# Two heads per tile in an attention backward kernel: 16 KB rows, and gradients written over their inputs

## The chip, the cores and the metric

The kernel runs on one core of a Trainium2 chip. A core has a matrix engine (TensorE, "PE" in the profile; its weight loads stand apart as "PEld"), a vector engine (VectorE, "DVE"), a scalar engine (ScalarE, "ACT"), GpSimd ("POOL") and SyncE ("SP"). Each runs its own list of instructions in order and waits on semaphores. Transfers between HBM and the on-chip memory (128 partitions) are issued here from SP and POOL, and a few from ACT; 16 DMA engines carry them all. The metric is the device time of one execution in microseconds: before the change the median of three runs is 402.32 us (402.08 to 402.48).

## The reference

The program is the forward and backward pass of a decode step: one query token attends over a cache of 32 heads, 4096 keys and 128 features per head, in parallel with a dense layer with a Mish activation, and a gate mixes the two. All arrays are bf16. Cut to what matters:

```python
def _A_ref(x, k_cache, v_cache, wq, wo):      # attention of one token
    q = (x @ wq).reshape(B, Sq, H, Dh).transpose(0, 2, 1, 3)
    scores = einsum("bhqd,bhkd->bhqk", q, k_cache) * (Dh ** -0.5)
    p = softmax(scores, axis=-1)
    o = einsum("bhqk,bhkd->bhqd", p, v_cache)
    return o.transpose(0, 2, 1, 3).reshape(B, Sq, H * Dh) @ wo

def _B_ref(x, w1, b1, w2):                    # dense layer: mish(x w1 + b1) w2
    h = x @ w1 + b1
    return (h * tanh(softplus(h))) @ w2

g = sigmoid((x * gate_w).sum(-1, keepdims=True))
out = g * _A_ref(A_x, K, V, wq, wo) + (1 - g) * _B_ref(B_x, w1, b1, w2)
# outputs: out, and the gradients of A_x, K, V, wq, wo, w1, b1, w2, gate_w
```

K and V are 32 MB each (32 heads of 1 MB), and so are their gradients dK and dV. dK of a head is the outer product of the vector ds (one number per key) with the query; dV is the outer product of the probabilities p with the gradient of the head's output. The weights wq and wo (5.2 MB each), w1 and w2 (2.2 MB each) are read, and gradients of their sizes are written.

## The kernel before, in words

**Tiles.** One head is one tile: 128 partitions, each holding J = 32 consecutive keys of 128 features, an unbroken row of 8 KB in HBM (the views `Kv`, `Vv`, `dKv`, `dVv`, L65 to L68). The pool `kv_in` has four K and four V tiles, the pool `outs` five tiles for dK and dV.

**The loop** (L749) goes over the 32 heads. `period(h)` (L645) does one head, and computes the scores of head h + 1 at its end. K and V come with the keys on the partitions, so each is turned by TensorE: `transposes` (L575) turns four blocks of 128x128 (bf16 pairs moved as f32) into a PSUM tile `tr`, and ScalarE copies it to `tT` (L582); `products` (L585) multiplies the result with the query (scores, tile `sA`) or with the output gradient (dP, tile `sB`). Then the softmax: `reduce_max` (L664), a transposition to spread the maximum (L668), `negM` (L670), the exponentials `e` (L675), their sum (L678, L680), `rz`, its reciprocal (L682), and `p_bf` (L684). `o_part` (L660) gives the head's output; `part`, `dd` and `ds` (L691 to L702) give the gradient of the scores; L713 gives the gradient of the query.

**dK and dV** are made by VectorE in `outer` (L602), half a head per instruction, four instructions per head: `dv_half(h, ...)` in the head's own period, `dk_half(h - 1, ...)` in the first part of the next one. After the second half the tile is stored, from POOL's queue (`ring`, L115), and by SP for the last two heads. Four dV tiles go out by `spread` (L637), in pieces of unequal partition counts.

**The order of the loads** is SP's list. At the start: wq, wo, K and V of the first three heads, w1, two parts of w2. Then, at the head of each pass of the loop, `load_k(h + 3)` and `load_v(h + 3)` (L757, L758): such a load waits until the tile's last reader is done. wo of the next groups of four heads and wq of the next eight are loaded from the same list (L753, L756).

**Everything else** (preparing a group of four heads in `prep_steps`, closing it in `finish_steps`, the dense layer in `mlp_steps`) is cut into steps with a kind: "P" mostly TensorE, "D" VectorE, "T" small. `slot` (L254), called three times per head, takes the first steps of the list whose predecessors were done in an earlier slot, two of kind P and one or two of kind D. This order is fixed when the program is built. At the end, the gradient of wq is made in five pieces (`dwq_make`, L729), in tiles of `kv_in`; the gradient of w1 is stored when head 31 is loaded (L759).

Of the kernel before, what the change touches and what calls it, by code (L numbers as in the profile page):

```python
# [16 lines left out]
def kernel(  # L17
# [25 lines left out]
    P = 128  # L43
# [3 lines left out]
    J = Sk // P  # L47
# [10 lines left out]
    CH = [(0, 5), (5, 9), (9, FCN)]  # L58
# [6 lines left out]
    Kv = A_k_cache.rearrange("b h (p j) d -> (b h) p j d", p=P)  # L65
    Vv = A_v_cache.rearrange("b h (p j) d -> (b h) p j d", p=P)
    dKv = out_2.rearrange("b h (p j) d -> (b h) p j d", p=P)
    dVv = out_3.rearrange("b h (p j) d -> (b h) p j d", p=P)  # L68
# [16 lines left out]
    KB, VB = 4, 4  # L85
    const = ctx.enter_context(tc.tile_pool(name="const", bufs=1))
    kv_in = ctx.enter_context(tc.tile_pool(name="kv_in", bufs=KB))
    outs = ctx.enter_context(tc.tile_pool(name="outs", bufs=5))
# [26 lines left out]
    def ring(h):  # L115
        return nc.sync if h >= H - 2 else nc.gpsimd

    def load_k(h):
        if h < H:
            kts[h] = kv_in.tile([P, J, Dh], BF16, name="Kn", tag="Kn", bufs=KB)  # L120
            nc.sync.dma_start(kts[h][:], Kv[h])

    def load_v(h):
        if h < H:
            vts[h] = kv_in.tile([P, J, Dh], BF16, name="Vn", tag="Vn", bufs=VB)
            nc.sync.dma_start(vts[h][:], Vv[h])
# [13 lines left out]
    def load_w2(c):  # L140
        a, b = CH[c][0], min(CH[c][1], FM)
        w2cs[c] = mlp.tile([P, 5, D], BF16, name="w2c", tag="w2c", bufs=2)
        nc.sync.dma_start(w2cs[c][:, 0:b - a, :], w2_v[:, a:b, :])
# [4 lines left out]
    load_v(0)  # L148
    load_k(1)
    load_v(1)  # L150
    load_wo(1)
# [6 lines left out]
    load_k(2)  # L158
    load_v(2)
# [3 lines left out]
    load_w2(1)  # L163

# [74 lines left out]
    for i in range(3):  # L239
        t = const.tile([P, 2, G, 2, 2], BF16, name=f"qd2_{i}")  # L240
        nc.gpsimd.memset(t[:], 0.0)
        qds.append(t)
    junk = const.tile([P, WG * Dh], BF16, name="junk")
# [25 lines left out]
    def prep_steps(g, head):  # L269
# [15 lines left out]
        def qbc():  # L285
            wq = wqs[g // 2]
            q_ps = gr_ps.tile([P, GD], F32, name="q_ps", tag="gr")
            for rc in range(RC):
                nc.tensor.matmul(q_ps[:], lhsT=x_bf[:, rc:rc + 1].to_broadcast([P, P]),  # L289
                                 rhs=wq[:, rc, off:off + GD], start=(rc == 0), stop=(rc == RC - 1))  # L290
            gp["qd"] = wts.tile([P, 2, GD], BF16, name="qd", tag="qd")
            nc.scalar.copy(gp["qd"][:, 0, :], q_ps[:])

        def dbc():
            d_ps = gr_ps.tile([P, G, P], BF16, name="d_ps", tag="gr")
            bcast_rows(d_ps, gp["do4b"], G)
            nc.scalar.copy(gp["qd"][:, 1, :].rearrange("p (a i) -> p a i", i=G), d_ps[:].rearrange("p i a -> p a i"))

        def qdcol():
            c_ps = gp["qdc"] = gr_ps.tile([P, 2, G], F32, name="c_ps", tag="gr")  # L300
            for w in range(2):
                for hh in range(G):
                    nc.tensor.matmul(c_ps[:, w, hh:hh + 1], lhsT=gp["qd"][:, w, hh * Dh:(hh + 1) * Dh],
                                     rhs=ident_bf[:, 0:1], start=True, stop=True)
# [7 lines left out]
        def x2():  # L312
# [5 lines left out]
            nc.scalar.mul(t[0:hf, :, :, :, 0], x2[0:hf], scale)  # L318
            nc.scalar.mul(t[hf:P, :, :, :, 1], x2[hf:P], scale)
# [78 lines left out]
    def mlp_steps():  # L398
# [107 lines left out]
        def dh_cast():  # L506
            m["dh_bf"] = T("dh_bf", BF16)
            nc.vector.tensor_copy(m["dh_bf"][:], m["dh"][:])
            m["dh_bc"] = mlp.tile([P, F], BF16, name="dh_bc", tag="dh_bc")
# [36 lines left out]
        for c in range(NCH):  # L546
# [5 lines left out]
            add(f"dw2a_{c}", "D", dw2_part(c, a, a + 3), (f"badd{c}",) + tuple(f"dh_{fc}" for fc in range(a, b)), H0)  # L552
            add(f"dw2_{c}", "D", dw2_part(c, a + 3, b), (f"dw2a_{c}",), H0)
# [10 lines left out]
        add("dhc", "T", dh_cast, (f"dh_{FCN - 1}",), H0)  # L564
        add("dhb0", "P", dh_bc_part(0), ("dhc",), H0)
        add("dhb1", "P", dh_bc_part(1), ("dhc",), H0)
        for rc in range(RC):
            for k in range(2):
                add(f"dxm{rc}_{k}", "D", dx_part(rc, k), ("dhb0", "dhb1"), H0)
            add(f"dw1_{rc}", "D", dw1_part(rc), (f"dxm{rc}_1",), H0)  # L570

# [13 lines left out]
    def products(out, tb, c, vec):  # L585
        for t in range(4):
            k = c * 4 + t
            for par in range(2):
                nc.tensor.matmul(out[:, 2 * k:2 * k + W], lhsT=tb[:, t, par, :],  # L589
                                 rhs=vec[:, par, :].unsqueeze(1).to_broadcast([P, W // 2, 2]),  # L590
                                 start=(par == 0), stop=(par == 1))

    def k_chunk(h, c, ts):
        ts.append(transposes(kts[h], c))

    def s_chunk(h, c, ts):
        gp = gps[h // G]
        if c == 0:
            sts[h] = {"A": sa_ps.tile([P, 512], F32, name="sA", tag="sA")}
        products(sts[h]["A"][:, 0:J + W], ts[c], c, gp["x2"][:, 0, h % G])  # L600

    def outer(dst, col, row, half):  # L602
        n = J // 2
        a, b = half * n, (half + 1) * n
# [6 lines left out]
    def dk_half(h, half):  # L611
        if h < 0:
            return
        st = sts[h]
        if half == 0:
            st["dK"] = outs.tile([P, J, Dh], BF16, name="dK_sb", tag="dVK")
        outer(st["dK"], st["ds"], gps[h // G]["qd"][:, 0, (h % G) * Dh:(h % G + 1) * Dh], half)
        if h == H - 1:
            a, b = half * (J // 2), (half + 1) * (J // 2)
            ring(h).dma_start(dKv[h][:, a:b, :], st["dK"][:, a:b, :])  # L620
        elif half == 1:
            ring(h).dma_start(dKv[h], st["dK"][:])  # L622
        if half == 1:
            sts.pop(h)

    def dv_half(h, half):
        st = sts[h]
        if half == 0:
            st["dV"] = outs.tile([P, J, Dh], BF16, name="dV_sb", tag="dVK")
        outer(st["dV"], st["p"], gps[h // G]["qd"][:, 1, (h % G) * Dh:(h % G + 1) * Dh], half)  # L630
        if half == 1:
            if h % 7 == 5 and h < H - 3:
                spread(h // 7, dVv[h], st["dV"])
            else:
                ring(h).dma_start(dVv[h], st["dV"][:])  # L635

    def spread(i, dst, t):  # L637
        src = t[:].rearrange("p j d -> p (j d)")
        out = dst.rearrange("p j d -> p (j d)")
        if i % 3 == 0:  # L640
            nc.gpsimd.inc_swdge_sem([], [], mode="reset_dge_cursor")
        for a, b in (((120, 125), (0, 120), (125, 128)), ((0, 14), (14, 119), (119, 128)), ((0, 8), (8, 128)))[i % 3]:
            nc.gpsimd.dma_start(out[a:b, :], src[a:b, :], max_dma_last_dim=J * Dh)

    def period(h):  # L645
        gp = gps[h // G]
        st = sts[h]
        nxt = h + 1 < H
        A = st["A"]
        S, Z, O, MM = A[:, 0:J], A[:, 96:96 + J], A[:, 128:128 + W], A[:, 256:384]  # L650
        B = st["B"] = sb_ps.tile([P, 512], F32, name="sB", tag="sB")
        DP, DQ, PT = B[:, 0:J + W], B[:, 128:128 + W], B[:, 256:384]
        vec = gp["x2"][:, 1, h % G]
        tv, tk = [], []
        V = lambda c: tv.append(transposes(vts[h], c))
        dP = lambda c: products(DP, tv[c], c, vec)

        def o_part(a, b):
            for j in range(a, b):
                nc.tensor.matmul(O, lhsT=vts[h][:, j, :], rhs=st["e"][:, j:j + 1].to_broadcast([P, W]),  # L660
                                 start=(j == 0), stop=(j == J - 1))

        m32 = small.tile([P, 1], F32, name="m32", tag="m32")
        nc.vector.reduce_max(m32[:], S, axis=AX.X)  # L664
        V(0)
        dk_half(h - 1, 0)
# [3 lines left out]
        nc.vector.tensor_reduce(negM[:], MM, axis=AX.X, op=ALU.max, negate=True)  # L670
        dk_half(h - 1, 1)
        e = st["e"] = small.tile([P, J], BF16, name="e_bf", tag="e_bf")
        V(2)
        dP(0)
        nc.scalar.activation(e[:], S, ACT.Exp, bias=negM[:], scale=1.0)  # L675
        V(3)
        dP(1)
        nc.tensor.matmul(Z, lhsT=ones_bf[:], rhs=e[:], start=True, stop=True)  # L678
        zs = small.tile([P, 1], F32, name="zs", tag="zs")
        nc.vector.reduce_sum(zs[:], Z, axis=AX.X)  # L680
        rz = st["rz"] = small.tile([P, 1], F32, name="rz", tag="rz")
        nc.vector.reciprocal(rz[:], zs[:])  # L682
        p_bf = st["p"] = small.tile([P, J, 2], BF16, name="p_bf", tag="p_bf")
        nc.scalar.activation(p_bf[:], e[:].unsqueeze(2).to_broadcast([P, J, 2]), ACT.Copy, scale=rz[:])  # L684
        dP(2)
        o_part(0, J)
        dP(3)
        slot(h)
        part = small.tile([P, 1], F32, name="part", tag="part")
        pj = small.tile([P, J], F32, name="pj", tag="pj", bufs=1)  # L690
        nc.vector.scalar_tensor_tensor(pj[:], in0=DP[:, 0:J], scalar=1.0, in1=e[:], op0=ALU.mult, op1=ALU.mult,  # L691
                                       accum_out=part[:])
        dv_half(h, 0)
        nc.tensor.transpose(PT, part[:].to_broadcast([P, P]), ident_f[:])  # L694
        if nxt:
            k_chunk(h + 1, 0, tk)
            k_chunk(h + 1, 1, tk)
        dd = small.tile([P, 1], F32, name="dd", tag="dd")
        dj = small.tile([P, P], F32, name="dj", tag="dj", bufs=1)
        nc.vector.tensor_scalar(dj[:], PT, rz[:], None, ALU.mult, ALU.add, accum_out=dd[:])  # L700
        ds = st["ds"] = small.tile([P, J, 2], BF16, name="ds_bf", tag="ds_bf")
        nc.vector.scalar_tensor_tensor(ds[:], in0=DP[:, 0:J].unsqueeze(2).to_broadcast([P, J, 2]), scalar=dd[:], in1=p_bf[:],  # L702
                                       op0=ALU.subtract, op1=ALU.mult)
        dv_half(h, 1)
        nc.vector.tensor_scalar(o_all[:, h:h + 1], O[:, 0:1], rz[:], None, ALU.mult)  # L705
        if nxt:
            s_chunk(h + 1, 0, tk)
            k_chunk(h + 1, 2, tk)
        slot(h)
        if nxt:  # L710
            s_chunk(h + 1, 1, tk)
        for j in range(J):
            nc.tensor.matmul(DQ, lhsT=kts[h][:, j, :], rhs=ds[:, j, 0:1].to_broadcast([P, W]),  # L713
# [141 lines left out]
```

## Time and profile before

| | |
|---|---|
| median of three runs | 402.32 us |
| the profiled execution's own time | 402.56 us |
| its span, first to last instruction | 400.8 us |
| VectorE busy | 303.1 us (76%), 783 instructions |
| TensorE busy, matmul / weight load | 301.0 us (75%) / 266.0 us (66%), 5752 each |
| ScalarE busy | 178.2 us (44%) |
| moved by DMA | 164.92 MB, mean 412 GB/s |
| K tile, issue to landing, median | 24.0 us |
| dK tile, issue to landing, median | 11.8 us |

The profile page gives, for one execution, the busy time of each engine, and the same cut into 40 slices of about 10 us each: one digit per slice and engine, in tenths. Below that stand the granted TensorE clock, the mean busy share of the 16 DMA engines, and the GB/s that they moved. Further parts list the DMA queues (q1 carries what SP issues, q0 what POOL issues), the chain of waits that ended last, and groups of instructions with their counts, total and mean times, and the idle time before them. A window of the trace can be asked for by itself; it gives the busy microseconds of each engine in it, the clock, the DMA share and the GB/s.

### The profile page before, as it was taken

To read this page: it belongs to the slowest core of one execution; us is meant where nothing else is said; L and a number is where in the kernel's file an instruction comes from. 1 tells how busy PE (TensorE), PEld (TensorE's weight loads), DVE (VectorE), ACT (ScalarE), POOL (GpSimd) and SP (SyncE) were. 2 spreads that over 40 slices of the span, in tenths; PEclk is the share of its full clock that TensorE was granted. 3 is DMA by queue.
4 is the path that set the end of the run, shared out by engine and by line. 5 is a ranking of instruction groups with operands and counts; after the bars stand their busy time and mean duration, and the time that the engine had idled before them with its cause. 6 is when DMAs were issued, how large, how long until landed. Compare 5 with 4: busy or idle time off the path is not lost.

```text
span 400.8 us, 13361 instructions
## 1 busy us (share of the span) xinstructions
PE 301.0 (75%) x5752; PEld 266.0 (66%) x5752; DVE 303.1 (76%) x783; ACT 178.2 (44%) x403; POOL 47.0 (12%) x94
## 2 busy tenths in 40 slices
PE   0788888678888788768879788838888888888300
PEld 0577888567777677658868778718777678877200
DVE  3339666556799999767658999836999997898860
ACT  1455454325545555326533555604545545555000
POOL 0001111021110111211110112101111121111000
PEclk9899999959999999969977999967999999999755
DMA  8999999999999999999999999999999999999995
GB/s 292 417 407 405 418 426 421 407 423 421 424 421 424 422 422 416 422 424 424 419 424 426 422 422 417 417 425 424 421 421 424 424 423 418 425 420 418 424 383 229
DMA packets 28359, 164.92 MB, mean 412 GB/s; under 512 B 3260, under 2 KB 3964, under 8 KB 12556
## 3 DMA queue, kind: packets, MB, share of 16 engines
q1 hardware_dynamic: 17136, 93.41, 56.5%
q0 software_dynamic: 11104, 70.64, 42.3%
q8 instruction: 45, 0.74, 0.7%
q14 instruction: 14, 0.11, 0.1%
q10 hardware_dynamic: 60, 0.01, 0.0%
HBM read 82.03 MB, written 82.03 MB: 409 GB/s over the span
## 4 chain that ended last, share of the span: by engine, by line
DVE 38%; DMA 32%; PE 20%; ACT 5%; issue 3%; ACTq 0%; SPq 0%
DMA Kn<-in_A_k_cache_dram 30%; DVE dK_sb L605 9%; DVE dV_sb L605 9%; PE tr L580 8%; DVE junk L378 5%; ACT tT L582 4%; DVE junk L278 3%; PE sA L660 3%; PE sA L589 3%; PE sB L713 3%; DVE junk L530 2%; DVE wo_g L367 1%; DMA vec_rows<-in_gate_w_dram 1%; DVE dj L700 1%; DVE dwq_t L732 1%
## 5 line engine op out<-in xcount | busy, mean ns | idle before, releaser
L582 ACT COPY tT<-tr 128x512 f32<-128x512 f32 x256 | 142.4, 587 | 127.8 <-PE tr L580 126.0
L589 PEld LDWEIGHTS <-tT 128*128 128x128 bf16 x2048 | 79.8, 98 | 40.3 <-ACT tT L582 34.6
L580 PE MATMUL tr<-ident_f,Kn 128*128 128x128 f32 x512 | 81.6, 297 | 9.2 <-DMA Kn<-in_A_k_cache_dram 9.2
L605 DVE TENSOR_TENSOR dV_sb<-p_bf,qd 128x2048 bf16<-128x2048 bf16 x64 | 78.0, 1218 | 0.2 <-issue 0.2
L605 DVE TENSOR_TENSOR dK_sb<-ds_bf,qd 128x2048 bf16<-128x2048 bf16 x64 | 77.7, 1216 | 0.0
L580 PE MATMUL tr<-ident_f,Vn 128*128 128x128 f32 x512 | 72.9, 278 | 0.0
L580 PEld LDWEIGHTS tr<-ident_f,Kn 128*128 128x128 f32 x512 | 61.0, 152 | 10.4 <-issue 10.4
L589 PE MATMUL sA<-qd,tT 128*128 128x48 bf16 x1024 | 48.7, 187 | 23.8 <-ACT dq_all L718 12.7
L580 PEld LDWEIGHTS tr<-ident_f,Vn 128*128 128x128 f32 x512 | 56.3, 142 | 0.0
L589 PE MATMUL sB<-qd,tT 128*128 128x48 bf16 x1024 | 46.0, 183 | 0.0
L660 PEld LDWEIGHTS <-Vn 128*128 128x128 bf16 x1024 | 30.2, 95 | 10.9 <-issue 10.9
L660 PE MATMUL sA<-e_bf,Vn 128*128 128x48 bf16 x1024 | 30.7, 183 | 8.1 <-DVE zs L680 6.5
L622 POOL DMA_DIRECT2D out_dram<-dK_sb x30 | 17.2, 574 | 138.9 <-DVE rz L682 86.5
L713 PE MATMUL sB<-ds_bf,Kn 128*128 128x48 bf16 x1024 | 32.2, 186 | 1.4 <-DVE ds_bf L702 1.4
L664 DVE TENSOR_REDUCE m<-sA 128x1 f32<-128x32 f32 x32 | 6.1, 189 | 32.9 <-PE sA L589 26.4
L713 PEld LDWEIGHTS <-Kn 128*128 128x128 bf16 x1024 | 29.5, 98 | 1.6 <-issue 1.6
L635 POOL DMA_DIRECT2D out_dram<-dV_sb x26 | 14.1, 542 | 135.8 <-DVE o_all L705 53.4
L278 DVE SCALAR_TENSOR_TENSOR junk<-wo_g,da_bc 128x640 bf16<-128x640 bf16 x32 | 26.2, 820 | 1.7 <-ACT da_bc L229 1.1
L378 DVE SCALAR_TENSOR_TENSOR junk<-wq_g,dq_bc 128x1024 bf16<-128x1024 bf16 (+1 forms) x25 | 25.1, 1005 | 0.2
L700 DVE TENSOR_SCALAR_CACHE_REDUCE dj<-sB,rz 128x128 f32<-128x128 f32 x32 | 11.1, 346 | 13.2 <-PE sB L694 13.2
L289 PE MATMUL q_ps<-wq_g,cols_bf 128*128 128x512 bf16 x40 | 13.1, 469 | 10.5 <-DMA wq_g<-in_A_wq_dram 10.5
L684 ACT ACTIVATE p_bf<-e_bf,rz 128x64 bf16<-128x64 bf16 x32 | 11.1, 348 | 13.9 <-DVE rz L682 11.1
(148 smaller groups left out, 268.8 us busy)
## 6 DMA issues: line engine op xcount, KB each, us to landing
Kn<-in_A_k_cache_dram SPq DMA_DIRECT2D x32, 1024.0 KB, 24.0
Vn<-in_A_v_cache_dram SPq DMA_DIRECT2D x32, 1024.0 KB, 28.0
out_dram<-dK_sb POOLq DMA_DIRECT2D x30, 1024.0 KB, 11.8
out_dram<-dV_sb POOLq DMA_DIRECT2D x26, 1024.0 KB, 11.8
wq_g<-in_A_wq_dram SPq DMA_DIRECT2D x4, 1280.0 KB, 23.2
wo_g<-in_A_wo_dram SPq DMA_DIRECT2D x8, 640.0 KB, 17.6
out_dram<-wo_g POOLq DMA_DIRECT2D x7, 640.0 KB, 11.8
out_dram<-dwq_t SPq DMA_DIRECT2D x4, 896.0 KB, 17.5
```

Of the source, the lines that this page charges most:

```text
L278: nc.vector.scalar_tensor_tensor(junk[:, 0:D], in0=wos[g][:, i, :], scalar=1.0, in1=da_bc[:], op0=ALU.mult, op1=ALU.mult, accum_out=gp["do ...
L289: nc.tensor.matmul(q_ps[:], lhsT=x_bf[:, rc:rc + 1].to_broadcast([P, P]), rhs=wq[:, rc, off:off + GD], start=(rc == 0), stop=(rc == RC - 1))
L378: nc.vector.scalar_tensor_tensor(junk[:, c0:c1], in0=wqs[w][:, rc, c0:c1], scalar=1.0, in1=dq_bc[:, w * WG * Dh + c0:w * WG * Dh + c1], op ...
L580: nc.tensor.transpose(tp[:, t, :], flat[:, k * P:(k + 1) * P], ident_f[:])
L582: nc.scalar.copy(sb[:].rearrange("p a b -> p (a b)"), tp[:].rearrange("p a b -> p (a b)"))
L589: nc.tensor.matmul(out[:, 2 * k:2 * k + W], lhsT=tb[:, t, par, :], rhs=vec[:, par, :].unsqueeze(1).to_broadcast([P, W // 2, 2]), start=(pa ...
L605: nc.vector.tensor_tensor(dst[:, a:b, :].rearrange("p j (a b) -> p j a b", b=2), col[:, a:b, :].unsqueeze(2).to_broadcast([P, n, Dh // 2, 2]),
L622: ring(h).dma_start(dKv[h], st["dK"][:])
L635: ring(h).dma_start(dVv[h], st["dV"][:])
L660: nc.tensor.matmul(O, lhsT=vts[h][:, j, :], rhs=st["e"][:, j:j + 1].to_broadcast([P, W]), start=(j == 0), stop=(j == J - 1))
L700: nc.vector.tensor_scalar(dj[:], PT, rz[:], None, ALU.mult, ALU.add, accum_out=dd[:])
L713: nc.tensor.matmul(DQ, lhsT=kts[h][:, j, :], rhs=ds[:, j, 0:1].to_broadcast([P, W]), start=(j == 0), stop=(j == J - 1))
```

## The change

A tile holds two heads. Partitions 0 to 63 hold head 2n, partitions 64 to 127 head 2n + 1, each partition J = 64 keys: rows of 16 KB, a tile of 2 MB. There are 16 such pairs; `period(n, mid)` does one. The number of blocks to turn and of products stays the same per head. The two heads share the 128 columns of a product, and each half of the partitions reads its own columns (`own`); the query and gradient vectors, `e`, and the new `dm` are laid out with zeros for the other head. Small VectorE and ScalarE steps of the softmax become one instruction per half (`HS`), and ScalarE gets two more copies per pair, from `dm` to `ds`.

dK is written over the K tile and dV over the V tile, in four instructions per pair and kind (`NQ`), of the same shape as before. The pool `outs` is gone; there are four K tiles and three V tiles of 16 KB per partition. A load into a tile is issued right after the store out of it (`load_k(n + 4)` at the end of `dk_part`, `load_v(n + 3)` at the end of `dv_part`), and so has to wait for that store.

The initial loads have another order, w2 comes in four parts instead of three, the gradient of w1 is stored as a step, two dV tiles go out by `spread` instead of four, and the pieces of the gradient of wq share three tiles.

```diff
-    J = Sk // P
+    HP = P // 2
+    J = Sk // HP
+    NP = H // 2
-    CH = [(0, 5), (5, 9), (9, FCN)]
+    CH = [(0, 4), (4, 7), (7, 10), (10, FCN)]
-    Kv = A_k_cache.rearrange("b h (p j) d -> (b h) p j d", p=P)
+    Kv = A_k_cache.rearrange("b (n two) (p j) d -> (b n) (two p) j d", two=2, p=HP)
...
-    KB, VB = 4, 4
+    KB, VB = 4, 3
-    outs = ctx.enter_context(tc.tile_pool(name="outs", bufs=5))
-    def ring(h):
-        return nc.sync if h >= H - 2 else nc.gpsimd
+    def ring(n):
+        return nc.sync if n == NP - 1 else nc.gpsimd
...
     load_k(0)
     load_v(0)
+    load_wo(1)
     load_k(1)
-    load_v(1)
-    load_wo(1)
     w1_sb = mlp.tile([P, RC, F], BF16, name="w1_sb", tag="w1_sb")
...
-    load_k(2)
-    load_v(2)
+    load_v(1)
     load_w2(0)
...
     load_w2(1)
+    load_k(2)
+    load_v(2)
+    load_k(3)
...
+            for k, hp in HS:
+                nc.scalar.copy(gp["qd"][hp, 0], q_ps[hp].rearrange("p (n k d) -> p n k d", n=2, k=2)[:, :, k, :])
...
+        def dw1_store():
+            nc.sync.dma_start(dw1_v, w1_sb[:])
+            stored.append(1)
+        add("dw1s", "T", dw1_store, (f"dw1_{RC - 1}",), 2 * (NP - VB))
...
+    def own(X, k, hp):
+        return X[hp, 0:2 * J].rearrange("p (a k r) -> p a k r", k=2, r=2)[:, :, k, :]
+    NQ = 4
+    def outer(dst, col, row, q):
+        n = J // NQ
...
+    def dk_part(n, q):
+        if n < 0:
+            return
+        st = sts[n]
+        outer(kts[n], st["ds"], gps[n // 2]["qd"][:, 0, n % 2, :], q)
+        if q == NQ - 1:
+            ring(n).dma_start(dKv[n], kts[n][:])
+            sts.pop(n)
+            kts.pop(n)
+            load_k(n + KB)
+    def dv_part(n, q):
+        st = sts[n]
+        outer(vts[n], st["p"], gps[n // 2]["qd"][:, 1, n % 2, :], q)
+        if q == NQ - 1:
+            if n in (3, 9):
+                spread(dVv[n], vts[n])
+            else:
+                ring(n).dma_start(dVv[n], vts[n][:])
+            vts.pop(n)
+            load_v(n + VB)
...
+    def period(n, mid):
+        for k, hp in HS:
+            nc.vector.tensor_reduce(m32[hp], own(S, k, hp), axis=AX.XY, op=ALU.max)
         V(0)
+        dk_part(n - 1, 0)
         V(1)
...
+        dk_part(n - 1, 3)
+        V(6)
+        dP(4)
+        slot(2 * n)
...
+        dv_part(n, 0)
+        K(0)
+        K(1)
...
+        dv_part(n, 1)
+        mid(n)
...
+        for k, hp in HS:
+            nc.scalar.copy(ds[hp], dm[hp, :, k].unsqueeze(2).to_broadcast([HP, J, 2]))
+        dv_part(n, 2)
+        slot(2 * n + 1)
+        SC(1)
+        K(3)
+        dv_part(n, 3)
...
+    def mid(n):
...
+        if n % 2 == 1:
+            load_wo(g + 2)
+            if g % 2 == 0:
+                load_wq(g // 2 + 1)
```

## The prediction

> **What bounds the kernel now.** I read the 40 slices first, for which resource is full; then the queues; then windows where one thing alone happens; then the waits.
>
> ```profile
> PE   0788888678888788768879788838888888888300
> DVE  3339666556799999767658999836999997898860
> PEclk9899999959999999969977999967999999999755
> DMA  8999999999999999999999999999999999999995
> GB/s 292 417 407 405 418 426 421 407 423 421 424 421 424 422 422 416 422 424 424 419 424 426 422 422 417 417 425 424 421 421 424 424 423 418 425 420 418 424 383 229
> DMA packets 28359, 164.92 MB, mean 412 GB/s; under 512 B 3260, under 2 KB 3964, under 8 KB 12556
> ...
> q1 hardware_dynamic: 17136, 93.41, 56.5%
> q0 software_dynamic: 11104, 70.64, 42.3%
> ```
>
> The DMA row is 9 in every slice but the first and the last; VectorE and TensorE, at 76% and 75% of the span, are not. The two data queues take 98.8% of the 16 engines' span. So bytes over rate set the time: 164.92 MB at 421 GB/s are 391.7 us, and the first slice (292) and the last two (383, 229) lose the rest.
>
> Windows, with the columns PE, PEld, DVE, ACT, POOL busy, granted clock, DMA share, GB/s:
>
> ```profile
> 20.00:25.00 5.00, 4.40 (x84) 4.05 (x83) 0.84 (x4) 3.15 (x7) 0.00 (x0) 0.96 1.04 402
> 265.00:275.00 10.00, 7.08 (x70) 5.16 (x70) 5.47 (x16) 2.34 (x4) 1.06 (x2) 0.50 1.02 428
> 282.00:371.50 89.50, 75.92 (x1547) 67.91 (x1543) 83.32 (x198) 47.23 (x107) 12.95 (x21) 1.00 1.01 421
> 380.00:386.00 6.00, 0.45 (x1) 0.18 (x1) 5.79 (x24) 0.00 (x0) 0.00 (x0) 0.50 1.01 425
> 386.00:395.00 9.00, 0.28 (x1) 0.09 (x1) 1.41 (x7) 0.25 (x1) 0.00 (x0) 0.50 0.87 352
> 395.00:398.00 3.00, 0.00 (x0) 0.00 (x0) 0.00 (x0) 0.00 (x0) 0.00 (x0) 0.50 0.54 206
> ```
>
> Rows of 3456 B (w1, 20 to 25 us) move at 402 GB/s, rows of 8 KB alone (265 to 275) at 428: a packet has a fixed cost. From 282 to 371.5 the compute runs without waiting for loads, VectorE 93% busy; the chain of waits shows a first dV instruction of a head at 282.16 and, nine heads on, at 371.51: 9.93 us a head, 19.9 a pair. After 386 the transfers run out unevenly.
>
> ```profile
> SPq L121 <- PE sB L713: 164.3, 20, 18.9
> ...
> Kn<-in_A_k_cache_dram SPq DMA_DIRECT2D x32, 1024.0 KB, 24.0
> Vn<-in_A_v_cache_dram SPq DMA_DIRECT2D x32, 1024.0 KB, 28.0
> out_dram<-dK_sb POOLq DMA_DIRECT2D x30, 1024.0 KB, 11.8
> ```
>
> SP waits 164 us for the last reader of a K tile, yet a load takes 24 to 28 us to land against 2.5 us for 1.05 MB at full rate: a deep queue stands before the engines. That queue is what the change must keep.
>
> **The change part by part.**
>
> *Rows of 16 KB.* Before: 8192 load rows and 7552 store rows of 8 KB, four dV tiles in 4 KB pieces (1024) and the last dK in two halves (256). After: 4096 loads, 30 stores of 128 rows (3840) and two dV tiles in 8 KB pieces (512). That is 8576 packets less. Their fixed cost: the packet records behind the DMA view give 309 ns for 8192 B and 159 ns for 4096 B, so 36.6 ns per KB and 9 ns fixed; 8576 x 9 / 16 engines = 4.8 us. The DMA share of 1.01 to 1.02 says that records overlap by some 1.2%, 3.7 ns of 309; with that taken off, 5.3 ns and 2.8 us. The two windows give 306.2 and 137.6 ns per packet and engine, 14.6 ns fixed, 7.8 us, but mix in other rows. I take 4.0, between the first two, which are of the same rows; ends 2.8 and 7.8.
>
> [...]
>
> *Fewer transfers.* Some 60 DMAs fewer, each ending in one 4 B record of 9 ns per engine: 0.5 us. Ends 0 and 0.6.
>
> *Compute per pair.* TensorE keeps its turns and products; dK and dV keep 8 instructions of 1.217 us a pair. Small VectorE steps, by the rows (m 189, negM 285, zs 186, rz 164, pj 190 + 83, dj 346 + 83, ds 284, o_all 215 ns) and 1 ns per column (a 32-column reduction takes 189, a 128-column one 285): before, two heads, 4.05 us; after 0.44 + 0.44 + 0.29 + 0.16 + 0.61 + 0.73 + 0.57 + 0.22 = 3.46. So 19.9 becomes 19.3 us. ScalarE gets two `ds` copies of about 0.4 us a pair (the p row is 348 ns) and, per group, six copies for two in the preparation, 7 us over the run; both on an engine that is 44% busy, while VectorE writes dV. All this lies beside the transfers: a middle pair moves 8.39 MB of K, V, dK, dV, 0.66 of wo and its gradient and 0.33 of wq, 9.37 MB or 22.0 us at 425 GB/s. Cost nothing while 19.3 is below 22.0; if that cover went, each us costs 16.
>
> *In place, loads behind stores.* SP now waits for a store to land before the load into that tile, and everything later in its list (the other load, wo, wq, w2) stands behind it; TensorE's turns of the next K (L580 of before), VectorE's `do_part` (L278) and the q products (L289) wait for those. By the places in VectorE's list, a K tile is held by compute from 0.6 of the pair before to 0.42 of the pair after, 1.8 of its 4 pair times; a V tile 0.85 of 3. That leaves 2.2 pair times of 22 us, 48 us, for a store and a load of 4.9 us each. Held in the DMA system: about 4.4 tiles or 9 MB, 21 us of work. Before: K 2.6 and V 3 heads ahead and up to three gradient tiles, 8.6 MB. The queue stays as deep, so value 0. From below, no gain is possible where the engines are already full; from above, see the rivals.
>
> *Start.* The prologue turns 8 chunks instead of 4, about 5 us later compute; the first dV store moves from 29.0 to about 42 us. Loads cover it: 20.7 MB are in the initial list, until 52 us. The first K tile has landed at 12.6 us (4.06 MB at 424 after the 3.1 us that the first slice loses), before the 16.7 us at which turning began. Value 0.
>
> *End.* The moved store of w1's gradient stands behind the last V load, ahead of the wq pieces on SP. After that load there are left: that store 2.2 MB, dK14, dV15, dK15 2.1 each, wq pieces 4.6 and 0.66, two wo gradients 1.3: 15.1 MB, 35.5 us. Compute: a pair 19.3, last dK 4.7, the closing steps 10.4 (377.8 to 388.2 in the chain), 2.5 for the last rows: 36.9. So the overhang is about 1.4 us; before, the end lost 5.8 us to uneven engines, which may stay. The last store is 2.1 MB rather than 0.52, 3.7 us if nothing covers it. I take +1.0; ends -2 and +3.7.
>
> *Sum.* 402.56 - 4.0 - 0.5 + 1.0 = 399.1 by the profiled execution; the median lies 0.24 below that, so 398.8.
>
> **The rivals.**
>
> *The rings run dry behind the weight loads (slower).* wo of the next group is queued behind two tiles of 2 MB. While VectorE waits for it no dV is written, so no V store goes, and only two loads, 9.8 us of work, are left; if the wait is longer, the engines idle, and then a landing and a fresh issue have to pass: the first issue ended at 1.17 us and the rate of the first slice says that data flowed from 3.1, so 1.9 us each. For it: in-order SP, and the 10.5 us that L289 already waits for wq. Against: stores land in 11.8 us while loads queue. Six such waits, wo 2 to 7, at 1.9 us are 11.4 us: 410.2.
>
> *Compute becomes the bound.* It decides from 22.0 us a pair. For it: VectorE is 93% busy in the free stretch, and the softmax chain has more instructions. Against: 2.7 us of room. At 23 us, 16 x 1.0 = 415.
>
> *No change.* A 16 KB row costs as much as two of 8 KB, or the end (+3.7) eats the gain: 402.3. For it: the 45 instruction packets of 16 KB took about 1 us each. Against: they are instruction fetches on a queue of their own, not rows of K or V.
>
> *A larger gain.* 14.6 ns per packet and an even end: 402.3 - 7.8 - 0.6 - 2 = 391.9.
>
> **How the numbers follow.** A measurement of this kernel tells 0.2% (0.8 us) from no change. Forecast 0.60, with its own range 395 to 401.4; larger gain 0.03; no change 0.10; dry rings 0.21; compute 0.06. Faster: 0.57 of the forecast and 0.03, with 0.02 of the no-change case: 0.62. Same: 0.03 + 0.06 = 0.09. The rest, 0.29, is slower. The range 395.0 to 410.5 leaves out the compute rival, about half of the larger-gain case and of the dry rings' tail, and a little below: under 0.2.
>
> **What would show it.** Right: DMA 9 in slices 2 to 38, some 19,000 packets, stretches of K and V alone at 430 GB/s or more, a pair of 22 us with TensorE waiting for loads. Dry rings: DMA digits of 7 or 8 every second pair, with VectorE waiting for wo in `do_part`. Compute: VectorE at 95% with DMA below 9 in all slices. Wrong at the end: DMA below 9 from about 360 us on. Wrong on rows: long stretches still at 424 to 428 GB/s.

## The result, and the profile after

The changed kernel takes 429.4 us (427.0 to 432.6) where the kernel before takes 402.4 us: a ratio of 1.068, interval 1.059 to 1.077. It is slower by 27 us; the forecast was 398.8 us, with a range to 410.5. A fourth execution, of 433.7 us, counts as a slow one and is left out, as such executions are from every time and difference below (with it the median is 431.0 us, the figure that the expectations use). The profiled execution took 429.4 us, its span 427.6 us.

The page of the changed kernel, VectorE's row, the DMA rows and the two data queues:

```profile
DVE  3318766456795899922779699852699999799984
...
DMA  8999999998999999999999999999997999997997
GB/s 305 428 416 399 426 428 420 418 428 348 355 292 379 391 380 382 414 406 430 426 346 355 426 397 382 265 384 425 412 382 271 405 418 380 426 427 321 422 409 304
DMA packets 18726, 164.89 MB, mean 386 GB/s; under 512 B 2140, under 2 KB 2844, under 8 KB 10220
...
q1 hardware_dynamic: 12240, 93.41, 54.7%
q0 software_dynamic: 6368, 70.64, 41.4%
```

The bytes are the same and the packets fell as counted (18,726; some 19,000 were forecast). But the GB/s row, flat at 421 before, now falls to 350, 290, 265 again and again, while the DMA row says 9 in most of these slices (8 at 348, 7 at 271, 321 and in the last). So the digit, the prediction's sign for dry rings, hardly showed the loss; the GB/s row did. Two windows of the changed kernel, with the columns of the prediction, show the two forms of it:

```profile
222.00:227.00 5.00, 4.34 (x86) 4.23 (x85) 4.88 (x11) 4.56 (x12) 0.00 (x0) 1.00 1.00 354
322.50:325.50 3.00, 3.00 (x82) 2.97 (x78) 2.96 (x6) 1.17 (x2) 0.53 (x1) 1.00 0.14 57
```

In the second the engines have almost nothing to move. In the first they are busy and slow. The packet records give the size of the slow form: summed over an engine, packets took 24.6 us longer than the usual packet of their size did (611 ns at the median for 16 KB; 309 for 8 KB before), against 5.0 us before. Time without a packet grew too: the two data queues take 96.1% of the span, where it was 98.8%, which leaves some 17 us an engine without a packet, where it was 5. By this estimate 20 us of slow packets and 12 us of idle time, less some 4 to 5 us that the long rows save, make up the 27 us.

The waits of the changed kernel (engine, line and what ended the wait: us in total, times, longest), first of all engines, then of SP alone:

```profile
PE q_ps L299 <- DMA wq_g<-in_A_wq_dram: 32.2, 3, 13.4
...
DVE junk L288 <- DMA wo_g<-in_A_wo_dram: 25.2, 5, 6.7
```

```profile
SPq L127 <- DMA out_dram<-Vn: 163.5, 14, 26.0
SPq L122 <- DMA out_dram<-Kn: 134.1, 12, 16.7
```

SP, which waited 164 us for readers of K before, now waits 298 us for stores to land. TensorE waits for wq at each of its three later loads, and VectorE for wo five times: 57 us together. Before, TensorE's for wq was the only such wait:

```profile
PE q_ps L289 <- DMA wq_g<-in_A_wq_dram: 10.5, 3, 5.6
```

The issues of the page (transfer, queue, count, KB each, median us from issue to landing):

```profile
Kn<-in_A_k_cache_dram SPq DMA_DIRECT2D x16, 2048.0 KB, 15.5
Vn<-in_A_v_cache_dram SPq DMA_DIRECT2D x16, 2048.0 KB, 14.7
out_dram<-Kn POOLq DMA_DIRECT2D x15, 2048.0 KB, 13.2
out_dram<-Vn POOLq DMA_DIRECT2D x13, 2048.0 KB, 12.9
```

Loads of twice the size land sooner than the loads of before (24.0 and 28.0 us), so less stands in front of them. Bytes times latency over the span gives an estimate of what is in flight for K, V, dK and dV: before, 32 x 1.049 MB x (24.0 + 28.0 + 11.8 + 11.8) / 400.8 = 6.3 MB; after, 16 x 2.097 MB x (15.5 + 14.7 + 13.2 + 12.9) / 427.6 = 4.4 MB. The prediction had 8.6 and 9.

### The profile page after: what moved, and what is told of

The parts are those of the page before. It is cut to its first block, busy times and chain, and to the rows that moved or that the text cites. A ratio compares the mean times of both kernels' runs of the same rounds, so it can differ in the third digit from the quotient of the medians.

```text
span 427.6 us, 13147 instructions
## 1 busy us (share of the span) xinstructions
PE 296.8 (69%) x5665; PEld 264.4 (62%) x5672; DVE 309.8 (72%) x736; ACT 200.4 (47%) x451; POOL 29.1 (7%) x66
## 2 busy tenths in 40 slices
DMA packets 18726, 164.89 MB, mean 386 GB/s; under 512 B 2140, under 2 KB 2844, under 8 KB 10220
## 4 chain that ended last, share of the span: by engine, by line
DVE 32%; issue 24%; DMA 19%; PE 16%; ACT 5%; POOL 2%; SPq 1%; ACTq 0%; POOLq 0%; DVEq 0%
DMA wq_g<-in_A_wq_dram 11%; DVE Kn L634 8%; PE tr L602 7%; DVE Vn L634 6%; DMA wo_g<-in_A_wo_dram 5%; DVE junk L394 3%; ACT tT L604 3%; DVE junk L288 3%; DMA out_dram<-Kn 2%; PE sA L611 2%; DVE junk L546 2%; PE sB L760 2%; DMA vec_rows<-in_gate_w_dram 1%; PE sA L724 1%; DVE wo_g L383 1%
## 5 line engine op out<-in xcount | busy, mean ns | idle before, releaser
L602 PE MATMUL tr<-ident_f,Kn 128*128 128x128 f32 x512 | 87.5, 304 | 0.0
L634 DVE TENSOR_TENSOR Vn<-p_bf,qd 128x2048 bf16<-128x2048 bf16 x64 | 78.1, 1221 | 1.0
L602 PE MATMUL tr<-ident_f,Vn 128*128 128x128 f32 x512 | 78.4, 283 | 0.2 <-issue 0.2
L634 DVE TENSOR_TENSOR Kn<-ds_bf,qd 128x2048 bf16<-128x2048 bf16 x64 | 77.5, 1219 | 0.9
L288 DVE SCALAR_TENSOR_TENSOR junk<-wo_g,da_bc 128x640 bf16<-128x640 bf16 x32 | 26.3, 823 | 26.9 <-DMA wo_g<-in_A_wo_dram 25.2
L299 PE MATMUL q_ps<-wq_g,cols_bf 128*128 128x512 bf16 x33 | 13.6, 538 | 33.5 <-DMA wq_g<-in_A_wq_dram 32.2
L760 PE MATMUL sB<-dm,Kn 128*128 128x48 bf16 x1024 | 33.2, 188 | 2.2 <-DVE dm L744 2.2
L724 PE MATMUL sA<-em,Vn 128*128 128x48 bf16 x1024 | 30.9, 183 | 2.5 <-issue 2.5
L299 PEld LDWEIGHTS <-cols_bf 128*128 128x128 bf16 x40 | 5.2, 131 | 39.0 <-issue 30.8
L687 DVE TENSOR_REDUCE m<-sA 64x1 f32<-64x64 f32 x32 | 7.1, 221 | 27.3 <-PE sA L611 27.1
L394 DVE SCALAR_TENSOR_TENSOR junk<-wq_g,dq_bc 128x1024 bf16<-128x1024 bf16 (+1 forms) x25 | 25.2, 1007 | 0.2
L303 ACT CAST qd<-q_ps 64x256 bf16<-64x256 f32 x16 | 5.9, 367 | 38.1 <-PE q_ps L299 37.9
L733 DVE SCALAR_TENSOR_TENSOR junk<-sB,em 64x64 f32<-64x64 f32 x32 | 7.1, 222 | 18.6 <-PE sB L611 10.7
L736 PE MATMUL sB<-ident_f,part 128*128 128x128 f32 x16 | 5.2, 324 | 21.7 <-DVE junk L733 21.7
## 6 DMA issues: line engine op xcount, KB each, us to landing
Kn<-in_A_k_cache_dram SPq DMA_DIRECT2D x16, 2048.0 KB, 15.5
Vn<-in_A_v_cache_dram SPq DMA_DIRECT2D x16, 2048.0 KB, 14.7
out_dram<-Kn POOLq DMA_DIRECT2D x15, 2048.0 KB, 13.2
out_dram<-Vn POOLq DMA_DIRECT2D x13, 2048.0 KB, 12.9
```

The costliest lines, as they stand in the source:

```text
L288: nc.vector.scalar_tensor_tensor(junk[:, 0:D], in0=wos[g][:, i, :], scalar=1.0, in1=da_bc[:], op0=ALU.mult, op1=ALU.mult, accum_out=gp["do ...
L394: nc.vector.scalar_tensor_tensor(junk[:, c0:c1], in0=wqs[w][:, rc, c0:c1], scalar=1.0, in1=dq_bc[:, w * WG * Dh + c0:w * WG * Dh + c1], op ...
L602: nc.tensor.transpose(tp[:, t, :], flat[:, k * P:(k + 1) * P], ident_f[:])
L634: nc.vector.tensor_tensor(dst[:, a:b, :].rearrange("p j (a b) -> p j a b", b=2), col[:, a:b, :].unsqueeze(2).to_broadcast([P, n, Dh // 2, 2]),
L687: nc.vector.tensor_reduce(m32[hp], own(S, k, hp), axis=AX.XY, op=ALU.max)
L724: nc.tensor.matmul(O, lhsT=vts[n][:, j, :], rhs=e[:, j, :].unsqueeze(1).to_broadcast([P, W // 2, 2]), start=(j == 0), stop=(j == J - 1))
```

## The experiments

Theory L: the order of SP's list. A load waits for a store to land, wo and wq stand behind it, the compute waits for them, and while it waits no gradient is stored, no tile comes free and the rings run empty. Against it stood R (the traffic and the rows of 16 KB themselves), S (the dV stores in uneven pieces), J (a ring that starts beside one that ran alone moves slowly at first), and later T (the rings take turns packet by packet, so that rows of 16 KB starve the 2 KB rows of wq). All runs were timed beside the kernel before, at 402.35 to 402.75 us.

**Weights on ScalarE's queue**

```diff
-            nc.sync.dma_start(wqs[w][:], wq_v[:, :, w * WG * Dh:(w + 1) * WG * Dh])
+            (nc.scalar if w else nc.sync).dma_start(wqs[w][:], wq_v[:, :, w * WG * Dh:(w + 1) * WG * Dh])
-            nc.sync.dma_start(wos[g][:], wo_v[g])
+            (nc.scalar if g > 1 else nc.sync).dma_start(wos[g][:], wo_v[g])
```

> The changed kernel, but wo of groups 2 to 7 and wq 1 to 3 are loaded from ScalarE's queue instead of SP's list, so that they no longer stand behind K and V loads that wait for a store to land. Theory L (the list: TensorE's 32.2 us of waiting for wq at the q products and VectorE's 25.2 us for wo, while which no store is made and the rings run dry): these waits fall below 8 us together and the time falls from 431 to 400 to 412. Theory R (the traffic itself: 16 KB packets and store-then-load in one tile make the packets slow, 24.6 us of mean engine time above their usual length): the waits go, but the time stays above 420.

Measured 455.9 us, ratio 1.128 (1.120 to 1.135): slower by another 27 us, outside the range of theory L. The waits for wo are gone, but wq took 44.3 us to land and TensorE waited 65.8 us for it. That brought up theory T, tested below.

**All of dV stored plainly**

```diff
-            if n in (3, 9):
-                spread(dVv[n], vts[n])
-            else:
-                ring(n).dma_start(dVv[n], vts[n][:])
+            ring(n).dma_start(dVv[n], vts[n][:])
```

> The changed kernel, but the dV tiles of pairs 3 and 9 go out as one plain store each instead of in three pieces of 5, 120 and 3 partitions. The longest stretches of slow packets lie at 116 to 135 and 266 to 280 us, just after these stores. If the pieces make them (theory S), the slow packets there go and the time falls by 5 to 10 us. If the slow packets come with any ring that starts beside another (theory J), or if theory L holds, the time moves by less than 3 us.

Measured 420.2 us, ratio 1.045 (1.041 to 1.048): 9 us less. That is what theory S expected, and a miss for theory L. The wait for wq stayed (34.7 us); that for wo fell from 25.2 to 20.0 us.

**dK and dV in tiles of their own** (three K and two V tiles, two for the gradients, two heads and 16 KB rows kept), first with the uneven pieces, then with the weights on ScalarE's queue as well, then with plain stores:

```diff
-    KB, VB = 4, 3
+    KB, VB = 3, 2
+    outs = ctx.enter_context(tc.tile_pool(name="outs", bufs=2))
-        outer(kts[n], st["ds"], gps[n // 2]["qd"][:, 0, n % 2, :], q)
+        if q == 0:
+            st["dK"] = outs.tile([P, J, Dh], BF16, name="dK_sb", tag="dVK")
+        outer(st["dK"], st["ds"], gps[n // 2]["qd"][:, 0, n % 2, :], q)
...
-            load_k(n + KB)
```

> The changed kernel with two heads per tile and 16 KB rows, but dK and dV go to two tiles of their own again; three K and two V tiles, the same memory. A load then waits for the tile's last reader, as before the change, not for a store. Theory L: SP's 298 us of waiting for stores become waits for readers, the weights come earlier, and the time is 400 to 415. Theory R with the blame on 16 KB rows: above 420. With only two V tiles, waits for V may appear (up to 10 us).

> Both: tiles of their own for dK and dV, and the weights from ScalarE's queue. Theory L: the rings stay full, the DMA row is 9 throughout and the time is 396 to 403, the gain of the rows (some 3 to 4 us of 402.4) then showing. Theory R: above 415.

> Two heads a tile and 16 KB rows, but dK and dV in two tiles of their own (three K and two V tiles) and all of dV stored plainly. If the spread stores and the in-place order cost separately (10 and 19 us of the 431): 400 to 404 us, no wait for wq or wo over 10 us, excess over the nominal packet times as in the kernel before. If both are one cause: 408 to 412 us.

Measured 411.7 us (ratio 1.025, 1.020 to 1.030), 455.7 us (1.130, 1.124 to 1.137) and 409.8 us (1.020, 1.016 to 1.024). Without writing in place 18 us come back, and the waits for wo are gone; the plain stores, worth 9 us in place, are worth 2 here, and the two intervals overlap. So the uneven pieces (S) show no cost of their own; the pair with the weights first, below, says the same. Why they cost 9 us in the changed kernel was not tried further. Both kinds of tile with the weights on ScalarE's queue end at 456 us, so that loss is another one.

**In place alone: one head a tile, rows of 8 KB, seven K and six V tiles of 1 MB**

```diff
-    KB, VB = 4, 4
+    KB, VB = 7, 6
-    outs = ctx.enter_context(tc.tile_pool(name="outs", bufs=5))
-        outer(st["dK"], st["ds"], gps[h // G]["qd"][:, 0, (h % G) * Dh:(h % G + 1) * Dh], half)
+        outer(kts[h], st["ds"], gps[h // G]["qd"][:, 0, (h % G) * Dh:(h % G + 1) * Dh], half)
...
+            load_k(h + KB)
```

> The kernel before (one head a tile, rows of 8 KB) with dK and dV written over K and V, seven K and six V tiles of 1 MB in place of four, four and five of their own: the in-place half of the change alone. Theory L (each load waits in SP's order for a store to land, and wo and wq stand behind such a load): slower than before, 408 to 420 us, waits for wq or wo of over 20 us. Theory T (rings take turns packet by packet, and 16 KB rows are what makes the small-row weight loads slow beside stores): the rows are still 8 KB, so 401 to 405 us.

Measured 414.9 us, ratio 1.030 (1.028 to 1.033), inside theory L's range. The waits of this kernel, of the rows that name the weights:

```profile
PE q_ps L292 <- DMA wq_g<-in_A_wq_dram: 43.4, 3, 19.9
...
DVE junk L281 <- DMA wo_g<-in_A_wo_dram: 21.3, 4, 17.5
```

Long rows and two heads are not needed for the effect; writing in place is enough for 12.5 us of it, of the 27 us of the whole change.

**Packets of 8 KB in the changed kernel** (each load and plain store issued as two halves of the row)

```diff
-            nc.sync.dma_start(kts[n][:], Kv[n])
+            two(nc.sync, kts[n], Kv[n], True)
+    def two(eng, t, hbm, load):
+        for a in (0, J // 2):
+            b = a + J // 2
...
```

> The changed kernel, each load of K or V and each plain store of dK or dV issued as two transfers of half a row, so that packets are of 8 KB again and the order stays. Theory T: a 2 KB row of wq then waits for one 8 KB packet of the other ring (309 ns) instead of one of 16 KB (611 ns), some 11 us less for each 1.31 MB: the waits for wq (32 us) and wo (25 us) about halve, 412 to 420 us. Theory L: the waits stay, and 8 KB rows cost some 4 us: 430 to 437 us.

Measured 427.4 us, ratio 1.058 (1.053 to 1.064), which overlaps the changed kernel's. It lies above T's range and below L's. The wait for wq was 38.3 us, that for wo 17.8: together as long as in the changed kernel (56 and 57 us). On SP's queue, theory T carries nothing that these runs can tell.

**The same packets with the weights on ScalarE's queue**

> Weights on ScalarE's queue (which took 44.3 us from issue to landing for wq, and 456 us in all) with K, V, dK and dV in packets of 8 KB. Theory T: on a ring of its own each of the 40 wq packets per engine waits for one packet of each other ring, 40 x (84 + 2 x 611) = 52 us with 16 KB and 40 x (84 + 2 x 309) = 28 us with 8 KB while both others run, so wq lands in 22 to 30 us and the whole takes 430 to 445 us. If turns are not taken by packets, 38 to 46 us and 450 to 460 us.

Measured 417.9 us, ratio 1.039 (1.035 to 1.042): 38 us less than with 16 KB, more than T expected, while wq took longer to land than its 22 to 30 us. The landing of wq, first with packets of 16 KB, then of 8 KB:

```profile
wq_g<-in_A_wq_dram ACTq DMA_DIRECT2D x3, 1280.0 KB, 44.3
```

```profile
wq_g<-in_A_wq_dram ACTq DMA_DIRECT2D x3, 1280.0 KB, 33.5
```

The packet records of the first such load (8 KB) show the turns: in its 26.4 us an engine moved 39.9 packets of wq, 37.5 of the store queue and 37.2 of SP's queue. Nearly one for one for one: in this load a ring with 2 KB rows got about a quarter of the bytes of a neighbour with 8 KB. A row counts as a packet here, as in the profile. The first such load beside 16 KB packets took 33.6 us, with 40.0, 21.4 and 28.1 packets: no even turns there, perhaps because the other rings did not always have one to send, which no run shows. So the even turns are shown for one load only. In direction T holds where the weights have a ring to themselves, and it is the likely reason why that remedy failed. It does not explain the changed kernel, whose wq needed only 5.6 to 13.4 us from first to last packet on SP's ring.

**Nobody waits for weights.** The loads keep bytes, order and rows, but land in a tile of their own; the steps use the first ones.

```diff
-            wqs[w] = wts.tile([P, RC, WG * Dh], BF16, name="wq_g", tag="wq_g")
+            wqs[w] = wts.tile([P, RC, WG * Dh], BF16, name="wq_g", tag="wq_d" if w else "wq_g", bufs=1)
             nc.sync.dma_start(wqs[w][:], wq_v[:, :, w * WG * Dh:(w + 1) * WG * Dh])
+            wqs[w] = wqs[0]
...
             nc.sync.dma_start(wos[g][:], wo_v[g])
+            wos[g] = wos[g % 2]
```

> The changed kernel with the same loads in the same order, but wq after the first and wo after the second group land in tiles that nobody reads; the steps work on the first ones instead, so these outputs hold other numbers. The traffic stays, the waits of TensorE and VectorE for weights go. Theory L: those waits are what empties the rings, so 404 to 412 us. Rival, that the rings empty because loads wait for stores whoever waits for weights: 422 to 431 us.

Measured 407.7 us, ratio 1.013 (1.012 to 1.015), inside theory L's range. The same transfers, 21.7 us less: that much of the loss hangs on the waits for weights, and not on the traffic or the rows (R). No wait for wq or wo is left in the profile, and the two queues take 98.3% of the span again, so the engines are hardly ever empty:

```profile
q1 hardware_dynamic: 12240, 93.41, 56.0%
q0 software_dynamic: 6368, 70.64, 42.3%
```

**Weights first.** One place in SP's list changed:

```diff
             kts.pop(n)
-            load_k(n + KB)
+            if n % 2:
+                load_k(n + KB)
...
                 load_wq(g // 2 + 1)
+            load_k(n - 1 + KB)
```

> The changed kernel with one place in SP's list changed: in every second pair the load of the next K tile, which waits for a store to land, is issued after wo and wq instead of before them; both are then in the rings some 10 us earlier, bytes and tiles stay. Theory L (taking the weight waits away altogether brought 431 to 407.7 us): the waits for wq and wo (32 and 25 us) shrink to under half, 412 to 421 us. If the waits are set by how slowly the weights move beside the stores (15 to 24 us from issue to landing) and not by their place: 425 to 433 us.

> The same with all of dV stored plainly instead of two tiles in three pieces. Plain stores alone saved 10 us; if that gain and the place of the weights are separate, 403 to 412 us; if the spread only hurt through weight waits, the same as with the weights first alone, 412 to 421 us.

Measured 408.2 us, ratio 1.013 (1.012 to 1.015), below the range expected, and 411.5 us (1.022, 1.018 to 1.026) with plain stores, which here gain nothing. SP's timeline (start, duration, transfer) of the changed kernel and of the one with the weights first:

```profile
58.40 0.33 SPq L127 DMA_DIRECT2D Vn<-in_A_v_cache_dram  x1
67.24 0.33 SPq L122 DMA_DIRECT2D Kn<-in_A_k_cache_dram  x1
67.61 0.48 SPq L137 DMA_DIRECT2D wo_g<-in_A_wo_dram  x1
68.14 0.46 SPq L132 DMA_DIRECT2D wq_g<-in_A_wq_dram  x1
```

```profile
57.04 0.33 SPq L127 DMA_DIRECT2D Vn<-in_A_v_cache_dram  x1
57.41 0.44 SPq L137 DMA_DIRECT2D wo_g<-in_A_wo_dram  x1
57.90 0.48 SPq L132 DMA_DIRECT2D wq_g<-in_A_wq_dram  x1
67.14 0.33 SPq L122 DMA_DIRECT2D Kn<-in_A_k_cache_dram  x1
```

In the changed kernel SP sits from 58.7 to 67.2 us at the K load, which waits for dK of an earlier pair; wo and wq, ready to go, stand behind it. Ten us earlier in the list is worth 21.2 us of time. The waits for wo all but vanish (25.2 to 0.8 us), those of TensorE for wq fall only from 32.2 to 23.5 us:

```profile
PE q_ps L299 <- DMA wq_g<-in_A_wq_dram: 23.5, 3, 10.0
```

What is left of these waits seems to cost little: the version in which nobody waits is only 0.5 us faster. So the length of a wait does not tell its price.

**Both removed: nobody waits for weights, and plain stores; then also with own tiles**

> The changed kernel with wq and wo landing in tiles that nobody reads (the outputs that need them hold other numbers) and all of dV stored plainly. If the weight waits and the spread stores are all that went against the forecast: 397 to 401 us, as forecast. If loads that wait for stores also empty the rings by themselves: 404 to 408 us.

> Two heads a tile, 16 KB rows, dK and dV in two tiles of their own, all stored plainly, and wq and wo landing in tiles that nobody reads (the outputs that need them hold other numbers). If only writing in place was left against the forecast: 397 to 401 us. If tiles of 2 MB in so small a number (three K, two V, two of their own) stall by themselves: 404 to 410 us.

Measured 409.0 us (ratio 1.016, 1.014 to 1.017) and 411.2 us (1.021, 1.020 to 1.023): each about 1 us above the range of its second alternative. With own tiles, taking away the last 13.6 us of waiting for wq gained nothing (409.8 us with it). The GB/s row and the one wait for a tile of the first:

```profile
GB/s 300 431 409 402 424 423 428 425 416 424 429 425 425 425 432 422 421 422 426 431 422 426 379 358 362 376 372 422 428 430 423 424 426 425 419 404 404 422 419 109
```

```profile
PE tr L604 <- DMA Vn<-in_A_v_cache_dram: 17.1, 1, 17.1
```

Up to the 22nd slice this is the forecast: slices 5 to 22 have a mean of 424.8 GB/s, against 421.3 in the same slices of before, 0.8% more. Then TensorE waits 17.1 us for one V load, and five slices of 358 to 379 follow, which cost some 6.6 us ((2120 - 1847) / 424 x 10.2).

**In place with 1 MB tiles, weights first (the edit is against the in-place version above); then with nobody waiting; and the control, the kernel before with nobody waiting**

```diff
-            load_v(h + VB)
+            if h % G != 2:
+                load_v(h + VB)
...
                 load_wq(g // 2 + 1)
+            load_v(h - 1 + VB)
```

> One head a tile, 8 KB rows, dK and dV in place (414.9 us with the weights behind a V load that waits for a store), now with wo and wq issued before that V load. Theory L: the wait for wq (43 us) falls under 20 us and the time to 402 to 406 us. If writing in place costs by itself: 408 to 415 us.

> One head a tile, 8 KB rows, dK and dV in place, with wq after the first and wo after the second group landing in tiles that nobody reads (the outputs that need them hold other numbers). If writing in place costs only through the weights: 401 to 404 us, and the 5 to 9 us left in the versions with two heads belong to their tiles of 2 MB. If writing in place costs by itself: 406 to 411 us.

> The kernel before with the same weights landing in tiles that nobody reads: the control. Its transfers are full throughout, so the 10.5 us that TensorE waits for wq cost nothing: 401.5 to 403 us. If these waits cost something there too: 396 to 400 us, and the versions without weight waits have to be set against that.

Measured 407.7 us (ratio 1.013, 1.012 to 1.015), 404.1 us (1.005, 1.003 to 1.007) and 402.4 us (1.000, 0.999 to 1.001). Weights first bring back 7.2 of 12.5 us here; the waits are still 36.3 us for wq and 18.2 for wo, and the time lies just below the range in which writing in place costs by itself, so this run reached only part of what was expected. Without weight waits, writing in place in 13 tiles of 1 MB costs 1.6 us. The control is as fast as the kernel before: there the same kind of wait is free.

**Halves by partition.** With the weights first, each tile was moved as two transfers of 64 partitions, one head each, rows still 16 KB, so that a load waits for half a store only.

```diff
+    def two(eng, t, hbm, load):
+        for a in (0, HP):
+            b = a + HP
...
```

> The changed kernel with the weights first (408.3 us), and each load and plain store of a K or V tile issued as two transfers of 64 partitions, one head each, rows still 16 KB: a load of the first half then waits only for the store of the first half. If the size of the step (a store of 2 MB lands 13 to 15 us after its issue before a load goes) is what is left: 398 to 404 us. If not: 406 to 412 us.

> The same with all of dV stored plainly. The pieces of the spread stores cost nothing once weights are first (408.3 with them, 411.5 without): within 3 us of the run with them, so 397 to 405 us if the size of the step is what is left, 406 to 413 if not.

Measured 527.3 us (ratio 1.311, 1.306 to 1.316) and 522.4 us (1.298, 1.294 to 1.301): 119 and 111 us slower than the same without halves. Windows with loads alone (PE, PEld, DVE, ACT, POOL busy, granted clock, DMA share, GB/s), of the changed kernel and of the first of these two:

```profile
10.00:15.00 5.00, 3.52 (x15) 1.65 (x15) 3.69 (x11) 1.59 (x4) 0.00 (x0) 1.00 1.01 429
```

```profile
8.00:12.00 4.00, 2.09 (x13) 1.35 (x13) 2.31 (x11) 1.05 (x3) 0.00 (x0) 1.00 1.02 210
12.00:20.00 8.00, 3.28 (x16) 1.75 (x15) 2.86 (x10) 1.95 (x8) 0.00 (x0) 1.00 1.02 215
```

The DMA share is full in both, at half the rate. The run therefore says nothing on the size of the step; that question stays open.

## Why the prediction was wrong

**The step that failed** is "In place, loads behind stores": "The queue stays as deep, so value 0." It took the time that compute holds a tile from the places in VectorE's list, and gave all the rest to the DMA system, 9 MB. The profile's latencies make it 4.4 MB: a tile also sits idle, loaded, while the compute waits for something else. That something is wo and wq. The step says itself that they stand behind the load in SP's list, but sets no issue time against a need: wq was issued at 68.1 us, was wanted by TensorE at 77.3 and came at 89.1 (start and duration, and in brackets the idle time before it):

```profile
89.12 0.59 PE L299 MATMUL q_ps<-wq_g,cols_bf 128*128 128x512 bf16 x1 [11.81 <-DMA wq_g<-in_A_wq_dram]
```

This place costs 21.2 us (moved) or 21.7 us (nobody waits). The 8.6 MB that the step set for before were 8.6 tiles of 1.049 MB, 9.0 MB; the latencies that it had at hand give 6.3.

**The rival "dry rings behind the weight loads" had the mechanism and too small a price.** It counted six waits of wo at 1.9 us each, its estimate for a landing and a fresh issue, 11.4 us and 410.2. There were eight, five for wo and three for wq, of 57 us in all; at 21.7 us that is 2.7 us a wait on average, though they are not alike: with the weights first, 23.5 us of waiting for wq remain at little cost. The rival left out wq, though 10.5 us of waiting for it stood in the profile of before, and took the loss of one wait to be the restart alone. "Stores land in 11.8 us while loads queue" spoke against it; it stayed nearly true (13 us), and did not help, because the weights were queued behind the store and the load.

**Rows of 16 KB, -4.0.** Right in kind. A 16 KB packet took 611 ns at the median, where two of 8 KB take 618, and undisturbed slices of the run without weight waits and with plain stores were 0.8% faster, an estimate of 3.3 us over the whole. No version kept the gain.

**Fewer transfers, start.** Half a microsecond for fewer transfers can't be told apart in these runs. The first dV store was issued at 42.5 us, as forecast (42).

**Compute per pair, 19.3 us.** Right within a microsecond: the two shortest distances between dV stores are 18.6 and 18.7 us; the others are 21.7 to 30.5. Compute was not the bound.

**End, +1.0.** Not separated. The last four slices of the changed kernel (321, 422, 409, 304) mix the end with the last stall.

**The sum as it came out:** 398.8 forecast, 21.7 for the weight waits, and 8.9 left between 398.8 and 407.7. Of these, 1.6 us were seen for writing in place with small tiles. The other 7, which count the forecast's gain of 4 for the rows as real, appear only with two heads a tile, in place or not (407.7, 409.0, 411.2 us without weight waits). That seven tiles of 2 MB are too few pieces, so that one late tile stalls the compute and then the rings, fits the late V tile above; it was argued, not shown. No version had more tiles of 2 MB, and the other way to smaller steps, halves by partition, had a cost of its own.

None of the versions is faster than the kernel before. With the weights first, the changed kernel takes 408.2 us and the one in place with small tiles 407.7; they are the fastest of those that compute every output.

## What to carry to other kernels

When a buffer is reused in place, its load inherits the landing of a store (298 us of waiting on SP here); put nothing behind such a load in the same engine's list that compute needs soon (21.2 us for wo and wq), and set each issue time against the time of need and the landing time that the profile shows. A wait that is free under full DMA engines (the control: 402.4 us with and 402.4 without) can be dear where the waiting engine is the one that frees the tiles (the changed kernel: 429.4 with and 407.7 without); only taking it away tells its price. Read starvation from the GB/s row (265 to 355 in four slices here), not from the busy digit (9 in each of the four), and compare bytes in flight before calling a queue "as deep".

## What the runs showed of the hardware that was not expected

Transfers over 64 partitions ran at 210 to 215 GB/s with all 16 engines busy (a DMA share of 1.02), against 429 over 128 partitions with rows of the same 16 KB (1.01). Why the rate halved was not tried and stays open.

The load of wq, with rows of 2 KB, landed later on a ring of its own, and later still beside larger packets: it took 44.3 us to land beside 16 KB packets, 33.5 beside 8 KB, and 20 to 25 in SP's own ring in the changed kernel (its three later loads, from issue to last packet).

In the changed kernel packets also slowed in places where one data ring alone had any: from 222 to 225 us only the store ring did, and its 16 KB packets went from 611 ns to 1208, twice as much (the last 16 of these 59 took 1208 to 1258 ns), though from 218 to 222 us, alone as well, it had a median of 620. In the run by halves the loads' 16 KB packets took about as long (medians of 1294 and 1259 ns in the two windows above). Why packets slow in this way (theory J is one answer) was not tried and stays open.
